# A new hand-written order for the first token group with its output layer, word buffers by need, and unmixed weight blocks sent to DRAM as soon as they are converted

## The chip, the cores and the metric

The kernel runs on one core of a Trainium2 chip, alone. A core has five engines, each of which works through its own instructions in order: TensorE (PE in the profile; PEld are its weight loads), VectorE (DVE), ScalarE (ACT), GpSimd (POOL) and SyncE (SP), which here only issues transfers (DMAs). They wait for one another by semaphores. The metric is the device time of one execution in microseconds (us).

## The reference

Inputs are q, k, v (float32) of 8 batches, 8 heads, 576 positions and 64 dimensions, and four weight matrices in float64. Attention runs within chunks of 64 positions; its output, as 4608 tokens of 512 features, goes through a layer that takes the largest of three products, and then through an output layer:

```python
scores = scale * np.matmul(q_c, k_c.transpose(0, 1, 2, 4, 3))
scores = scores - np.max(scores, axis=-1, keepdims=True)
attn = np.exp(scores)
attn = attn / (np.sum(attn, axis=-1, keepdims=True) + 1e-09)
out = np.matmul(attn, v_c)
...
h = np.maximum(np.maximum(x @ w1, x @ w2), x @ w3)
return (h @ w_out).astype(np.float32)
```

Here w1 to w3 are 512 x 768 and w_out is 768 x 512.

## The kernel before

**Tiles and groups.** The 4608 tokens are 36 tiles of 128. Two groups of four tiles come first (group 0 is tiles 0 to 3, group 1 is tiles 4 to 7), then four units of seven tiles. A float32 product is made of three reduced-precision ones (`three`, L154 to L157): each operand is split into a high part and the rest, and low times high, high times low and high times high are added in one PSUM bank. Three such matmuls are called a step.

**Groups 0 and 1** multiply plainly. The 768 hidden columns are six blocks j, each with three weights w; a block (j, w) is four steps over 512 tokens. After each of the three, the largest so far is kept (`maximum`, L289), and after the third the result is split (`high`, `low`, L297 and L303). The output layer (`onto`, L307) takes six steps for each tile, and `output` (L313) copies a tile out and stores it.

**The units** replace eight products by seven on operands that are sums of blocks. Their weights, nine sets (jp, w), are prepared once by `store` (L338): GpSimd adds high and low parts back together (L348) and forms four mixed blocks (L361), ACT and DVE split these (L366, L369), and SP writes one set as four transfers of unmixed blocks (`originals`, L371, 0.75 MB) and one of mixed blocks (`mixed`, L379, 1 MB). The units read them back through a ring.

**Attention of one tile** (`plain_steps`, L185) is a chain: load q and k (q), scores (S, PE, L205), maximum (mx, DVE, L210), subtract (sub, DVE, L215), exponential (exp, ACT, L219), sum (DVE, L163), add the small constant (eps, L166), reciprocal (rec, L169), normalize (nrm, DVE or GpSimd, L172), transpose (T, PE, L228), copy (at, ACT, L233), load v (v), times v (V, PE, L240), and for groups the split of the result (xh on ACT, L247; xl on DVE, L251). The scores of two tiles share one PSUM tile `s`, so S of a tile is held until sub of the tile before is done.

**Weights are converted** from float64 words on the chip. For each of 24 blocks (18 of w1 to w3 and six of w_out, which have j = 6) `piece` (L108) has seven operations: W loads 0.5 MB of words, A (ACT, L131) scales the upper word into a value buffer `ao`, B (ACT, L136) scales the lower word, C (DVE, L140) shifts, X (L144, DVE or GpSimd) adds, H (ACT, L147) takes the high part and Y (L150, DVE or GpSimd) the rest. X ends the use of the words, Y that of the value buffer.

**What sets the order.** The scheduler doesn't reorder: each engine gets its instructions in the order in which the program makes them. Group 0's hidden layer, all weight conversions and the attention of tiles 0 to 7 stand in the table `FIRST` (L44), one name for each operation: `q0`, `S0`, `T0` and so on for attention, `W01` for the words of block (0, 1), `h00a` for the product of block (0, 0) over columns 0 to 255 (b: 256 to 511, f: all), `F`, `hh` and `hl` for maximum, high and low, `i18` for 18 filler matmuls (L549). A `p` at the end puts the operation on GpSimd. Behind it, the output layer of group 0, group 1 and the units are loops of steps (L662 on); around these a planner places the remaining work by due times. `tiles` (L610) plans the attention of later tiles by `TABLE` (L32), and `stores` (L618) the nine sets, one each 7.2 us. `now` is its clock, which a step moves on by 0.68.

Of the kernel before, what the change touches and what calls it, by code (L numbers as in the profile page):

```python
# [20 lines left out]
P = 128  # L21
# [13 lines left out]
OPERANDS = 0.3  # L35

# [20 lines left out]
xh6 h52f F50f X65 X64p F51f H65 xh7 F52f H64 Y65 hh5f xl7 Y64 hl5f xl6
# [4 lines left out]
def chunk_attn_maxout_kernel(  # L62
# [44 lines left out]

    def piece(j, w):  # L108
# [18 lines left out]
        def exponent():  # L127


            st["a"] = ao_p.tile([P, 512], F32, name="ao", tag=f"ao{k % 4}")  # L130
            nc.scalar.activation(out=st["a"], in_=words(U32)[:, :, 1].bitcast(F32), func=AF.Prelu, scale=2.0 ** -112,  # L131
                                 alpha=2.0 ** 32)
# [52 lines left out]
    def plain_steps(t, x_of, col):  # L185
# [49 lines left out]
        def values():  # L235
            st["x"] = x = bank_of("ps_x")[:, :, t % 2] if t < 8 else bank_of("ps_s")[:, :, 1]
# [23 lines left out]
    def attention(t, x_of, col, norm):  # L260
# [3 lines left out]
        return [(at, pe, steps[name]) for name, at, pe in TABLE]  # L264
# [3 lines left out]
    def moe(t0, x_of, banks_in=((ps_m, "pm"),)):  # L268
# [386 lines left out]
    with tc.manual_schedule(engines={ET.PE, ET.DVE, ET.Activation, ET.Pool, ET.SP}):  # L655
# [4 lines left out]
        for g_ in groups:  # L660
            g_["places"][:] = places
# [46 lines left out]
```

## Time and profile before

| What | Value |
|---|---|
| median of 3 runs | 652.01 us (651.69 to 654.13) |
| the profiled execution | 654.27 us |
| its span, from first to last instruction | 652.5 us |
| granted TensorE clock, mean | 0.995 |
| moved by DMA | 133.70 MB, 205 GB/s over the span |
| median from issue to landing, q and k | 7.2 us |
| median from issue to landing, v | 6.7 us |
| median from issue to landing, mixed blocks | 5.1 us |
| group 0 with its output layer ends | 101.1 us |
| group 1's hidden layer ends | 170.8 us |

A line of the timeline gives start, duration, engine, line of the program, operation, what is written and read, and the count; in brackets the idle time before it and who ended that. A line of the view of waits gives who waited for whom, the total, the count and the longest. A line of the windows gives the stretch, its length, the busy time (and count) of PE, PEld, DVE, ACT and POOL, the granted clock, the share of the DMA engines and GB/s.

### The profile page before, as it was taken

To read this page: it belongs to the slowest core of one execution; us is meant where nothing else is said; L and a number is where in the kernel's file an instruction comes from. 1 tells how busy PE (TensorE), PEld (TensorE's weight loads), DVE (VectorE), ACT (ScalarE), POOL (GpSimd) and SP (SyncE) were. 2 spreads that over 40 slices of the span, in tenths; PEclk is the share of its full clock that TensorE was granted. 3 is DMA by queue.
4 is the path that set the end of the run, shared out by engine and by line. 5 is a ranking of instruction groups with operands and counts; after the bars stand their busy time and mean duration, and the time that the engine had idled before them with its cause. 6 is when DMAs were issued, how large, how long until landed. Compare 5 with 4: busy or idle time off the path is not lost.

```text
span 652.5 us, 12394 instructions
## 1 busy us (share of the span) xinstructions
PE 635.6 (97%) x5111; PEld 544.5 (83%) x5113; DVE 411.9 (63%) x667; ACT 235.0 (36%) x400; POOL 202.8 (31%) x179
## 2 busy tenths in 40 slices
PE   7899999889999999999999999999999999999997
PEld 3687888667889888888898898898989888999986
DVE  5897854588556767690585768348676761666520
ACT  5777733244332323352132424323242431112121
POOL 2431186675132323330323232123323321222200
PEclk9899999899999999999999999999999999999999
DMA  9844619998547575154576635346765341556311
GB/s 341 311 165 152 206 38 352 333 332 307 228 161 283 210 299 216 76 225 162 170 299 218 267 130 226 112 162 248 269 249 205 138 168 57 211 218 226 112 49 64
DMA packets 35911, 133.70 MB, mean 205 GB/s; under 512 B 3984, under 2 KB 6288, under 8 KB 30096
## 3 DMA queue, kind: packets, MB, share of 16 engines
q1 hardware_dynamic: 35856, 132.92, 55.1%
q8 instruction: 40, 0.66, 0.4%
q14 instruction: 15, 0.12, 0.1%
HBM read 106.95 MB, written 25.95 MB: 204 GB/s over the span
## 4 chain that ended last, share of the span: by engine, by line
PE 80%; DVE 8%; DMA 5%; ACT 4%; SPq 1%; issue 1%; POOL 0%; ACTq 0%; DVEq 0%
PE pm L155 25%; PE pm L156 24%; PE pm L157 24%; PE s L240 2%; PE s L205 2%; PE tp L228 2%; DMA buf<-in_vb 2%; DMA buf<-in_qk 1%; DMA w<-s 1%; DVE e L215 1%; DVE most L472 1%; DVE mx L210 1%; DVE pm L463 1%; DVE s L369 1%; DMA xl<-in_w 1%
## 5 line engine op out<-in xcount | busy, mean ns | idle before, releaser
L155 PE MATMUL pm<-X,ring 128*128 128x448 f32 x504 | 188.9, 375 | 0.0
L157 PE MATMUL pm<-X,ring 128*128 128x448 f32 x504 | 184.2, 365 | 0.0
L156 PE MATMUL pm<-X,ring 128*128 128x448 f32 x504 | 184.2, 365 | 0.0
L460 DVE TENSOR_TENSOR kept<-pm,kept 128x448 f32<-128x448 f32 x72 | 44.6, 620 | 101.4 <-PE pm L157 101.4
L466 POOL TENSOR_TENSOR kept<-kept 128x448 f32<-128x448 f32 x36 | 41.5, 1153 | 214.9 <-DVE kept L460 147.8
L155 PEld LDWEIGHTS pm<-X,ring 128*128 128x128 f32 x504 | 94.6, 188 | 8.8
L157 PEld LDWEIGHTS pm<-X,ring 128*128 128x128 f32 x504 | 94.7, 188 | 7.8
L156 PEld LDWEIGHTS pm<-X,ring 128*128 128x128 f32 x504 | 94.8, 188 | 7.1
L457 ACT COPY kept<-pm 128x448 f32<-128x448 f32 x72 | 38.3, 532 | 97.9 <-PE pm L157 94.0
L156 PE MATMUL pm<-wol,H 128*128 128x512 f32 x168 | 65.4, 389 | 0.0
L155 PE MATMUL pm<-woh,H 128*128 128x512 f32 x168 | 65.4, 389 | 0.0
L157 PE MATMUL pm<-woh,H 128*128 128x512 f32 x168 | 65.4, 389 | 0.0
L155 PE MATMUL pm<-xh,wl 128*128 128x512 f32 (+1 forms) x156 | 61.6, 395 | 0.0
L156 PE MATMUL pm<-xl,wh 128*128 128x512 f32 (+1 forms) x156 | 59.4, 381 | 0.3 <-DVE xl L251 0.3
L157 PE MATMUL pm<-xh,wh 128*128 128x512 f32 (+1 forms) x156 | 59.0, 378 | 0.0
L463 DVE TENSOR_TENSOR pm<-pm,kept 128x448 f32<-128x448 f32 x72 | 45.1, 626 | 12.4 <-PE pm L157 12.4
L172 POOL TENSOR_TENSOR e<-e,sm 128x512 f32<-128x512 f32 x23 | 24.1, 1046 | 71.6 <-DVE sm L169 48.0
L472 DVE TENSOR_TENSOR most<-pm,most 128x448 f32<-128x448 f32 x72 | 44.8, 622 | 2.2
L210 DVE TENSOR_REDUCE mx<-s 128x8 f32<-128x512 f32 x36 | 24.8, 688 | 31.2 <-ACT stage L254 24.6
L478 ACT CAST H<-most 128x448 fp32r<-128x448 f32 x48 | 26.9, 568 | 45.9 <-DVE most L472 45.7
L233 ACT COPY xs<-tp 128x512 f32<-128x512 f32 x36 | 21.1, 585 | 56.2 <-PE tp L228 56.2
L219 ACT ACTIVATE e<-e 128x512 f32<-128x512 f32 x36 | 22.8, 633 | 47.6 <-DVE e L215 47.6
(82 smaller groups left out, 969.7 us busy)
## 6 DMA issues: line engine op xcount, KB each, us to landing
ring<-w SPq DMA_DIRECT2D x36, 1024.0 KB, 6.7
ring<-w SPq DMA_DIRECT2D x36, 768.0 KB, 4.5
buf<-in_qk SPq DMA_DIRECT2D x36, 512.0 KB, 7.2
buf<-in_vb SPq DMA_DIRECT2D x36, 256.0 KB, 6.7
out_x<-ao SPq DMA_DIRECT2D x36, 256.0 KB, 2.1
w<-s SPq DMA_DIRECT2D x9, 1024.0 KB, 5.1
buf<-in_w SPq DMA_DIRECT2D x10, 512.0 KB, 3.8
buf<-in_wout SPq DMA_DIRECT2D x6, 512.0 KB, 3.4
```

The lines of the kernel that those rows point to most:

```text
L155: nc.tensor.matmul(out=o, lhsT=al, rhs=bh, start=first, stop=False)
L156: nc.tensor.matmul(out=o, lhsT=ah, rhs=bl, start=False, stop=False)
L157: nc.tensor.matmul(out=o, lhsT=ah, rhs=bh, start=False, stop=last)
L172: eng.tensor_tensor(out=e, in0=e, in1=sm.unsqueeze(2).broadcast_to([P, 8, 64]), op=ALU.mult)
L210: nc.vector.tensor_reduce(out=st["mx"].rearrange("p (g c) -> p c g", c=2), in_=st["s"], axis=AX.X, op=ALU.max)
L219: nc.scalar.activation(out=st["e"], in_=st["e"], func=AF.Exp, scale=SCALE)
L457: return lambda: nc.scalar.copy(out=kept(k), in_=o[i])
L460: return lambda: nc.vector.tensor_tensor(out=kept(k), in0=o[i], in1=kept(q), op=plus)
L463: return lambda: nc.vector.tensor_tensor(out=o[i] if w else M(j, c), in0=o[i], in1=kept(k), op=plus)
L466: nc.gpsimd.tensor_tensor(out=kept(2), in0=kept(2), in1=kept(1), op=plus)
L472: return lambda: nc.vector.tensor_tensor(out=M(j, c), in0=of(), in1=M(j, c), op=most)
L478: nc.scalar.copy(out=hh[j][:, c * half:(c + 1) * half], in_=M(j, c))
```

## The change

The program is changed in six places.

1. `FIRST` is another table. It loads q of tile 0 ahead of the first words, has 26 filler matmuls instead of 37, puts 23 operations on GpSimd instead of 17, and now holds the output layer of group 0 too (`P` with tile and block for its steps, `O` with the tile for the store), among the last blocks and the attention of tiles 5 to 7. `Z` opens the two further PSUM banks for products, which came only behind the table before; `M` starts the planner's work on the mixed sets.
2. `K` with a set's numbers writes the unmixed blocks of that set. It stands in the table, among the last weight blocks and the output steps; before, `store` planned it at 0.5 us into each set.
3. Word buffers: nine rooms, of which each W takes the first that is free in the table's order and each X gives one back (the rooms in the x tiles of group 1 only until those are needed). Before, the room was fixed by the block's number. Value buffers are handed out in the same way by A and Y.
4. Tiles 4 to 7 use the two halves of the bank pair `s` for S and for V, as later tiles do; before, they used the pairs `s` and `x` as tiles 0 to 3.
5. `LATER` moves T and at of the tiles that are prepared during group 1 by 1.4 us, and V and x by 2.8 us.
6. In the units, `high` and `low` of a finished block come 0.6 us later.

The planner's clock starts at -10.0 at `M` and runs on through the names P, S, T and V of the table. Nothing is added to or left out of the arithmetic.

```diff
+MIX = 0.5
+LATER = {"T": 1.4, "at": 1.4, "V": 2.8, "x": 2.8}
...
 FIRST = """
-W01 W02 q0 A01 C01 W10 A02 B02 C02 B01 q1 X02 i18 S0 X01 H02 q2 H01 Y02 A10 Y01p mx0 B10 sub0 q3 i5 S1 C10 exp0 sum0
...
+q0 i13 W01 A01 S0 i5 mx0 q1 sub0 W00 C01 exp0 sum0 S1 mx1 sub1 B01 q2 A00 exp1 W12 eps0 v0 q3 i8 rec0 B00 X01p S2 sum1
...
+P12 P33 xh6 xl6 P02 Y64 P13 Y65 P34 P14 P35 V7 P24 P03 K21 P25 P04 xh7 O2 P15 P05 K02 O0 xl7 O3 O1
...
+    words_in, values_in = {}, {}
+    free, rooms_of_words, x1 = list(range(9)), list(range(4)), False
+    for name in FIRST.split():
+        k = (3 * int(name[1]) + int(name[2])) if name[0] in "WAXY" else None
+        if name[0] == "W":
+            words_in[k] = free.pop(0)
+        elif name[0] == "A":
+            values_in[k] = rooms_of_words.pop(0)
+        elif name[0] == "Y":
+            rooms_of_words.append(values_in[k])
+        elif name[0] == "X":
+            free += [words_in[k]] if words_in[k] > 3 or not x1 else []
+        elif name[:2] == "xh" and int(name[2]) > 3 and not x1:
+            x1, free = True, [n for n in free if n > 3]
...
-            if k < 4 or 6 <= k < 10:
-                n = k if k < 4 else k - 6
-                st["r"] = early[n // 2][:, n % 2]
+            n = words_in[k]
+            if n < 7:
+                st["r"] = early[0][:, n] if n < 2 else early[1][:, n - 2] if n < 4 else early[2][:, n - 4]
             else:
-                st["r"] = att.tile([P, 512], I64, name="buf", tag="aa" if k in (20, 22) else ("qs", "rv")[k % 2], bufs=1)
+                st["r"] = att.tile([P, 512], I64, name="buf", tag=("qs", "rv")[n - 7], bufs=1)
...
-            st["s"] = s = bank_of("ps_s")[:, :, t % 2 if t < 8 else 0]
+            st["s"] = s = bank_of("ps_s")[:, :, t % 2 if t < 4 else 0]
...
-            st["x"] = x = bank_of("ps_x")[:, :, t % 2] if t < 8 else bank_of("ps_s")[:, :, 1]
+            st["x"] = x = bank_of("ps_x")[:, :, t % 2] if t < 4 else bank_of("ps_s")[:, :, 1]
...
-        return [(at, pe, steps[name]) for name, at, pe in TABLE]
+        return [(at + later.get(name, 0.0), pe, steps[name]) for name, at, pe in TABLE]
...
-        return [(0.0, whole(0, a)), (1.1, whole(1, b)), (0.5, originals), (2.2, sum_of(0, a21, a22, plus)),
+        ops[f"K{jp}{w}"] = originals
+        return [(0.0, whole(0, a)), (1.1, whole(1, b)), (2.2, sum_of(0, a21, a22, plus)),
...
-                return ops + ([(at + 0.8, high(j, c)), (at + 1.7, low(j, c))] if w == 2 else [])
+                return ops + ([(at + 1.4, high(j, c)), (at + 2.3, low(j, c))] if w == 2 else [])
...
+    early.append(stage_p.tile([P, 3, 512], I64, name="stage"))
...
+    for tt in range(4):
+        for j in range(JT):
+            ops[f"P{tt}{j}"] = lambda a=(tt, j): g0["onto"](*a)
+        ops[f"O{tt}"] = lambda tt=tt: g0["output"](tt)
+    mixing = [store(n) for n in range(len(sets))]
...
+            elif name == "Z":
+                more_banks()
+            elif name == "M":
+                running = True
+                stores()
             else:
                 ops[name]()
+            if running and name[0] in "PSTV":
+                passed(STEP)
...
-    groups, parts = [g0], [("do", lambda: stores()), ("steps", lambda: g0["project"](0, 1, 2, 3, before=4))]
+    groups, parts = [g0], []
...
-                for at, pe, fn in attention(t0 + tt, stage, tt * P, nc.gpsimd if u else nc.vector):
+                for at, pe, fn in attention(t0 + tt, stage, tt * P, nc.gpsimd if u else nc.vector, {} if u else LATER):
...
-            for at, fn in store(n):
-                plan(now + 6.0 + 7.2 * n + at, 0.0, fn)
+            for at, fn in mixing[n]:
+                plan(now + MIX + 7.2 * n + at, 0.0, fn)
...
-    now = -4 * JT * STEP - 2.0
+    now = -10.0
```

**The start of the program.** SP's first transfers before the change (`xh` and `xl` are rooms for words in the x tiles, `in_qk` holds q and k of a tile, `in_vb` its v):

```order
L122 DMA xh_128<-in_w123 128x512
L122 DMA xl_129<-in_w123 128x512
L193 DMA buf_137<-in_qk 128x1024
L122 DMA xl_129<-in_w123 128x512
L193 DMA buf_148<-in_qk 128x1024
L193 DMA buf_189<-in_qk 128x1024
L193 DMA buf_201<-in_qk 128x1024
```

and after it:

```order
L211 DMA buf_136<-in_qk 128x1024
L140 DMA xh_128<-in_w123 128x512
L211 DMA buf_180<-in_qk 128x1024
L140 DMA xh_128<-in_w123 128x512
L211 DMA buf_210<-in_qk 128x1024
L140 DMA xl_129<-in_w123 128x512
L215 DMA buf_217<-in_vb 128x512
```

The first q moved from third place to the first, one word block comes between each two loads of q, and v of tile 0 comes ahead of the fourth q. GpSimd's first work on weights and attention before (`ao` is a value buffer, `e` the exponentials of a tile, `sm` their sums; L144 is X, L150 is Y, L172 is nrm):

```order
L150 TENSOR_TENSOR wl0_120<-ao_139,wh0_114 128x512
L144 TENSOR_TENSOR ao_193<-ao_193,xl_129 128x512
L144 TENSOR_TENSOR ao_296<-ao_296,xh_128 128x512
L172 TENSOR_TENSOR e_316<-e_316,sm_343 128x512
L150 TENSOR_TENSOR wl1_121<-ao_193,wh1_115 128x512
```

and after (L162 is X, L190 nrm, L168 Y):

```order
L162 TENSOR_TENSOR ao_153<-ao_153,xh_128 128x512
L190 TENSOR_TENSOR e_182<-e_182,sm_187 128x512
L190 TENSOR_TENSOR e_207<-e_207,sm_249 128x512
L162 TENSOR_TENSOR ao_212<-ao_212,xh_128 128x512
L190 TENSOR_TENSOR e_266<-e_266,sm_319 128x512
L168 TENSOR_TENSOR wl0_120<-ao_212,wh0_114 128x512
```

All of the first three tiles' normalizations are GpSimd's now, where tiles 0 and 1 were DVE's, and the low part of block (0, 0), which stood on DVE, is sixth in its row.

**Group 1.** SP's transfers around the loads of q for tiles 8 and 9 before (`w1_1243`, `w2_1305` and `w3_1388` are sets in DRAM, `s_1288` mixed blocks, `out_x` the output):

```order
L193 DMA buf_1272<-in_qk 128x1024
L317 DMA out_x<-ao_1274 128x512
L374 DMA w2_1305<-wh0_114 128x512
L374 DMA w2_1305<-wl0_120 128x512
L376 DMA w2_1305<-wh1_115 128x256
L376 DMA w2_1305<-wl1_121 128x256
L380 DMA w1_1243<-s_1288 128x2048
L197 DMA buf_1320<-in_vb 128x512
L193 DMA buf_1330<-in_qk 128x1024
L374 DMA w3_1388<-wh2_116 128x512
L374 DMA w3_1388<-wl2_122 128x512
```

and after:

```order
L335 DMA out_x<-ao_1281 128x512
L211 DMA buf_1288<-in_qk 128x1024
L399 DMA w1_1029<-s_1301 128x2048
L215 DMA buf_1328<-in_vb 128x512
L211 DMA buf_1338<-in_qk 128x1024
L399 DMA w2_1269<-s_1371 128x2048
```

The unmixed blocks (L374 and L376) are gone from this stretch. On TensorE, the scores and the transpose around one tile of group 1 stood side by side before (`s<-buf` is S, `tp<-ident` is T, `s<-xs` is V):

```order
L205 MATMUL s<-buf 64x64 x16
L228 MATMUL tp<-ident,e 128x128 x4
L155 MATMUL pm<-xh,wl_122 128x512
L156 MATMUL pm<-xl,wh_116 128x512
L157 MATMUL pm<-xh,wh_116 128x512
```

and after, V and the scores of two tiles on stand side by side, and T comes three steps later:

```order
L258 MATMUL s<-xs,buf 64x64 x16
L223 MATMUL s<-buf 64x64 x16
L173 MATMUL pm<-xh,wl_122 128x512
L174 MATMUL pm<-xl,wh_116 128x512
L175 MATMUL pm<-xh,wh_116 128x512
```

T, which stood right behind S of the next tile, now has three steps ahead of it, and V comes four steps behind T instead of three.

More of the change, by code (lines that the diff above doesn't have):

```diff
@@ L35 @@
 OPERANDS = 0.3
+MIX = 0.5
+LATER = {"T": 1.4, "at": 1.4, "V": 2.8, "x": 2.8}
 FIRST = """
-W01 W02 q0 A01 C01 W10 A02 B02 C02 B01 q1 X02 i18 S0 X01 H02 q2 H01 Y02 A10 Y01p mx0 B10 sub0 q3 i5 S1 C10 exp0 sum0
-X10p W00 S2 mx1 eps0 sub1 v0 rec0 exp1 nrm0 sum1 i8 T0 v1 S3 mx2 at0 eps1 A00 rec1 nrm1 q4 B00 C00 i6 T1 sub2 V0 at1
-exp2 W12 mx3 X00p sum2 V1 xh0 W21 eps2 rec2 H10 sub3 nrm2p H00 xl0 v2 S4 xh1 Y00 exp3 Y10p xl1 W20 A12 T2 sum3 B12
-h00a eps3 v3 rec3 at2 C12 nrm3 A21 h01a B21 q6 C21 A20 X12 T3 V2 at3 W11 C20 H12 B20 X21 W30 V3 xh2 Y12p mx4 F00a xl2
@@ new lines @@
+H01 mx2 eps1 nrm0p T0 at0 rec1 v1 sub2 nrm1p V0 T1 exp2 C00 S3 X00p xh0 q4 W02 at1 B12 sum2 H00 eps2 V1 rec2 mx3 xh1
+nrm2p sub3 T2 S4 xl0 exp3 xl1 sum3 at2 Y00p v2 B02 W10 eps3 rec3 v3 nrm3 A02 W20 h00a V2 A12 C02 W31 T3 Y01p A10 xh2
+X02 H02 at3 C10 W11 C12 X12p F00a h01a Y02 V3 xl2 B10 xh3 B31 q5 X10p xl3 A20 W21 A11 h02a F01a H12 F02a B11 C11 W61
+W52 Z B20 B21 W40 H10 mx4 sub4 hh0a exp4 W22 C20 X20 W32 Y12 X11 Y10 A31 H11 W30 h01b hl0a h00b C31 h02b A21 H20 X31
+S5 F00b C21 Y11 h12f F01b A40 q6 v4 H31 sum4 W41 B40 X21p h10f F02b H21 Y31 Y20 B30 hh0b eps4 hl0b Y21 C40 mx5 B61
@@ L282, in products @@
             xh, xl = x_of()
-            ps[j, w] = bank()
+            ps[j, w, lo] = bank()
             for ct in range(CT):
-                three(ps[j, w][:, :n], wh[j][:, w, ct, :], wl[j][:, w, ct, :], xh[:, ct, cols], xl[:, ct, cols],
+                three(ps[j, w, lo][:, :n], wh[j][:, w, ct, :], wl[j][:, w, ct, :], xh[:, ct, cols], xl[:, ct, cols],
                       ct == 0, ct == CT - 1)
@@ L330, in hidden @@
                 [(1.1, lambda: high(j, 0, 512)), (1.8, lambda: low(j, 0, 512))] if w == 2 else [])
-        return dict(products=products, maximum=maximum, high=high, low=low, hidden=hidden, project=project, places=places)
+        return dict(products=products, maximum=maximum, high=high, low=low, hidden=hidden, project=project, places=places,
+                    onto=onto, output=output)
     minus, plus, most = ALU.subtract, ALU.add, ALU.max
@@ L555, in first_group @@
     def first_group():
+        nonlocal now
+        running = False
         for name in FIRST.split():
@@ L562, in first_group, with passed @@
                 ops[name](nc.vector)
+            elif name == "Z":
[3 more added lines that the diff above has]
+                stores()
             else:
                 ops[name]()
+            if running and name[0] in "PSTV":
+                passed(STEP)
     due = []
+    def passed(step):
+        nonlocal now
+        now += step
+        while due and due[0][0] <= now:
+            _, _, pe, fn = heapq.heappop(due)
+            fn()
+            now += pe
     def plan(at, pe, fn):
@@ L667, in chunk_attn_maxout_kernel @@
                 step, after = after if isinstance(after, tuple) else (STEP, after)
-                now += step
                 for at, fn in after:
-                    plan(now + at, 0.0, fn)
-                while due and due[0][0] <= now:
-                    _, _, pe, fn = heapq.heappop(due)
-                    fn()
-                    now += pe
+                    plan(now + step + at, 0.0, fn)
+                passed(step)
         while due:
```

35 lines of the change are left out of this document (17 added, 18 removed).

## The prediction

> **What bounds the kernel now.** I read the page's engine and clock lines first, then the view of who waited for whom, for TensorE alone, in two stretches.
>
> ```profile
> PE 635.6 (97%) x5111; PEld 544.5 (83%) x5113; DVE 411.9 (63%) x667; ACT 235.0 (36%) x400; POOL 202.8 (31%) x179
> PEclk9899999899999999999999999999999999999999
> ```
>
> TensorE is the bound: it is busy for 97% of the span, and the next engine for 63%. The clock digits dip to 8 twice, in the second slice and the eighth (a slice is 16.3 us). Time can only come from the places where TensorE idles, runs at a lower clock or does filler work. The waits from 0 to 101 us come first, those from 100 to 172 us behind the dots; what waits there are later lie in stages that the change leaves in their order.
>
> ```profile
> PE s L205 <- DVE e L215: 3.3, 3, 1.6
> PE pm L549 <- DVE h L551: 1.5, 1, 1.5
> PE tp L228 <- DVE e L172: 1.2, 2, 0.6
> PE tp L228 <- POOL e L172: 1.1, 1, 1.1
> ...
> PE s L205 <- DMA buf<-in_qk: 2.5, 1, 2.5
> PE tp L228 <- DVE e L172: 1.9, 2, 1.4
> ```
>
> The columns are total, times and longest. Scores (S, L205) and transposes (T, L228) wait for the softmax chain; the 1.5 us of L549 is the start of the program; one S waits 2.5 us for a transfer. These waits sum to 11.5 us, so they aren't all: filler and clock come on top. The landmarks and the pace of TensorE come from its timeline.
>
> ```profile
> 1.46 5.88 PE L549 MATMUL pm<-h 128*128 128x512 bf16 x18 [1.46 <-DVE h L551]
> ...
> 22.68 0.58 PE L156 MATMUL pm<-xl,wh 128*128 128x256 f32 x1 [0.28 <-DVE xl L251]
> 30.98 0.69 PE L205 MATMUL s<-buf 64*64 64x64 f32 x32 [0.56 <-DVE e L215]
> 31.61 0.38 PE L155 MATMUL pm<-xh,wl 128*128 128x256 f32 x1
> 32.26 0.28 PE L155 MATMUL pm<-xh,wl 128*128 128x256 f32 x1
> 32.61 0.28 PE L155 MATMUL pm<-xh,wl 128*128 128x256 f32 x1
> 37.81 0.50 PE L155 MATMUL pm<-xh,wl 128*128 128x512 f32 x1
> 44.75 0.39 PE L155 MATMUL pm<-xh,wl 128*128 128x512 f32 x1
> 45.43 0.39 PE L155 MATMUL pm<-xh,wl 128*128 128x512 f32 x1
> 60.32 0.66 PE L228 MATMUL tp<-ident,e 128*128 128x128 f32 x4 [1.07 <-POOL e L172]
> 60.73 0.48 PE L155 MATMUL pm<-xh,wl 128*128 128x512 f32 x1
> 101.06 0.39 PE L155 MATMUL pm<-xh,wl 128*128 128x512 f32 x1
> 170.81 0.39 PE L155 MATMUL pm<-woh,h 128*128 128x512 f32 x1
> ```
>
> The columns are start and duration; many rows between are left out. Starts show the pace, since matmuls overlap: a step of three products costs 45.43 - 44.75 = 0.68 us at 512 columns (a block of four steps 2.72) and 0.35 at 256 (a half block 1.4); an S costs 0.63 (30.98 to 31.61), and V, with the same 32 small matmuls, is taken alike; a T costs 0.41 (60.32 to 60.73). The first half block runs from 22.68, the full blocks of group 0 from 37.81, group 1 from 101.06, and its output layer from 170.81.
>
> From 22.68 to 37.81 the work is 6 half blocks (8.4), two S and three V (3.15) and two T (0.8): 12.4 us in 15.1. From 37.81 to 101.06 it is 15 blocks and 24 output steps (84 steps, 57.1), one S, three V and three T (3.75): 60.9 in 63.3, so only 2.4 is lost there, 1.1 of it the POOL wait and 1.3 the cost of seven insertions, 0.2 each. From 101.06 to 170.81 it is 72 steps (49.0) and seven tiles' S, V and T (11.7): 60.7 in 69.8. Nearly all that can be won lies **before 37.81 and between 101 and 171**.
>
> **Term 1: the start, up to the first half block.** The same work precedes it in both kernels (S0 to S4, T0 to T2, V0, V1); the order and the suppliers change. The rows that price the chain:
>
> ```profile
> 4.45 0.67 ACT L131 ACTIVATE ao<-xh 128x512 f32<-128x512 f32 x1 [2.44 <-DMA xh<-in_w]
> 8.12 1.03 PE L549 MATMUL pm<-h 128*128 128x512 bf16 x4 [0.16 <-issue]
> 8.88 0.68 DVE L210 TENSOR_REDUCE mx<-s 128x8 f32<-128x512 f32 x1
> 9.60 0.69 DVE L215 TENSOR_TENSOR e<-s,mx 128x512 f32<-128x512 f32 x1
> 10.33 0.63 ACT L219 ACTIVATE e<-e 128x512 f32<-128x512 f32 x1 [0.35 <-DVE e L215]
> 10.35 1.16 PE L205 MATMUL s<-buf 64*64 64x64 f32 x64 [1.21 <-DVE e L215]
> 10.99 0.69 DVE L163 TENSOR_REDUCE sm<-e 128x8 f32<-128x512 f32 x1 [0.36 <-ACT e L219]
> 19.92 0.20 DVE L169 RECIPROCAL sm<-sm 128x8 f32<-128x8 f32 x1
> 20.29 1.04 POOL L172 TENSOR_TENSOR e<-e,sm 128x512 f32<-128x512 f32 x1 [1.49 <-DVE sm L169]
> 28.64 1.29 POOL L150 TENSOR_TENSOR wl<-ao,wh 128x512 fp32r<-128x512 f32 x1 [5.62 <-ACT wh L147]
> ```
>
> The first transfer, a weight block, lands at 4.45. Now the first is q0, of the same size, so S0 waits only for its fillers: 13 instead of 18, which ended at 1.46 + 5.88 = 7.34. The last five run at full pace (four in 1.03 with their overlap, some 0.22 each): 7.34 - 1.1 = 6.2 for S0. Each link of the softmax chain takes 0.72 (mx to sub, 8.88 to 9.60), 0.73 (sub to exp), 0.66 (exp to sum) and 0.75 (sub to the next S, as S1 waits for sub0); S to mx I take as 0.76. By hand through the DVE's new order: S1 8.4; sum0 9.1, mx1 9.7, sub1 10.4; S2 11.2; sum1 11.8, mx2 12.4, rec1 13.2.
>
> Then GpSimd carries the path. Its new order there is X01p, nrm0p, nrm1p, X00p, nrm2p, Y00p: three normalizations (1.04 each; two of them were the DVE's) and three conversion steps (1.29 each). X01p starts near 9.6 behind B01, nrm0p at 11.5; nrm1p follows rec1 by 0.37 (19.92 to 20.29) at 13.6; X00p ends at 15.9, nrm2p at 17.0, Y00p at 18.3. The first half block needs Y00's low words, so it can start at **18.3**; xl1 on the DVE is due at the same time. I take 18.7, for collisions between DVE and GpSimd. Before, the order made it wait until 22.68, so the gain is **4.0**. Bounds: 4.7 with nothing in the way; 2.7 if each of the six GpSimd steps is late by 0.2.
>
> **Term 2: 18.7 to the full blocks.** Six half blocks (8.4), S5, T3, V2 and V3 (2.3) and four insertions (0.8) make 11.5, plus 0.7 for a slow clock, which the row below shows for before as well: at 72% of 5 us, 1.4 us of pace went missing.
>
> ```profile
> 20.00:25.00 5.00, 3.99 (x48) 3.49 (x49) 4.79 (x12) 4.56 (x9) 2.73 (x2) 0.72 0.93 323
> ```
>
> That is 12.2, to 30.9. From there 84 steps (57.1), two S, four V and four T (5.4) and ten insertions (2.0) make 64.5: **95.4**. For waits that the trace can't show (the conversions of ACT and DVE stay close behind TensorE, output steps stand between the last blocks, tiles 4 to 7 share one bank pair) I add 1.0, from bounds of 0 and 4.0; 4.0 is over twice the 1.6 of softmax waits (0.56, 1.07) that the old order had after its first half block. Group 0 with its output ends at **96.4 instead of 101.06: 4.7**. The five banks that Z opens early can only take waits away. Word buffers by need cost no instruction; W21 to W30 are issued once a conversion frees a room, by my walk 5 us or more before ACT wants them, so that queue hides itself, as long as a transfer lands in some 5 us.
>
> **Term 3: group 1.** Seven tiles are prepared here while nine mixed weight sets are written to DRAM.
>
> ```profile
> 105.00:110.00 5.00, 5.00 (x52) 3.95 (x51) 1.30 (x2) 1.06 (x1) 4.66 (x5) 1.00 1.05 370
> 115.00:120.00 5.00, 2.50 (x40) 1.96 (x39) 1.46 (x3) 0.00 (x0) 3.90 (x4) 0.78 1.03 405
> 108.76 0.92 SPq L193 DMA_DIRECT2D buf<-in_qk  x1
> 118.17 1.13 PE L205 MATMUL s<-buf 64*64 64x64 f32 x32 [2.50 <-DMA buf<-in_qk]
> 119.23 1.11 PE L228 MATMUL tp<-ident,e 128*128 128x128 f32 x4
> 121.34 0.39 PE L155 MATMUL pm<-xh,wl 128*128 128x512 f32 x1
> ```
>
> The DMA engines are full (share 1.03 to 1.05), and q9, issued at 108.76, holds S9 until 118.17: 2.5 us idle. The clock then drops: S, T and one step take 121.34 - 118.17 = 3.17 where they should take 1.72, so 1.45 more. Per tile, one set brings 0.75 MB of unmixed blocks, 1 MB of mixed ones and 0.75 MB of q and v. The change writes the unmixed blocks in group 0, so 0.75 of 2.5 MB goes: at 370 GB/s a tile's transfers fall from 6.8 to 4.7 us, below its seven-microsecond share of the stretch. In SP's queue q9 then has only w1 and v8 ahead of it. I take all 3.95. LATER puts T 1.4 us and V 2.8 us later, which removes the T waits (1.9, longest 1.4); behind a waiting T stand only matmuls with operands at hand; the load of v for the tile after next shares V's buffer and now waits for V in SP's queue, about 1 us, with the next q behind it. That gives 5.85; I keep 5.0, as one wait of some 0.9 may come back (the loads of q have little lead). Bounds: 1.9, if q9 is late anyway, and 5.85.
>
> The unmixed blocks now stand in SP's queue between the last word and v loads: nine times four transfers, 6.75 MB or 18 us at 370 GB/s, beside some 10 us for what else moves there, in about 30 us. Nothing computed waits for them, and TensorE's own work hides them; without that cover, 0 to 18 us.
>
> In the units, high and low now come 0.6 us later. Before the output layer reaches those rows 12 steps (8.2 us) pass, so that costs 0.
>
> **Sum.** 4.7 + 5.0 = 9.7. From the profiled span of 652.5 that gives 642.8; the execution lasted 654.27, 1.8 beyond its span, and the median of the runs is 652.01. Against that median I predict **642.3**.
>
> **Rivals.** *Conversions bind group 0:* DVE is busy for 4.79 of 5 us in the row from 20 to 25. If ACT and DVE can't keep up when TensorE starts earlier, the 4.7 shrinks to about 1.0: 652.0 - 6.0 = 646.0. Against it: each word block's instructions are the same, and six more of them, net, run on GpSimd.
>
> *The clock in the start:* 11 fillers go (37 to 26). After the last one at 10.8 TensorE has some 4.5 us of work in 8. If it then runs slow for most of that, S takes 1.06 as at 118.17 (to 119.23) instead of 0.63 and T is drawn out alike, some 2.5 more for the chain to 18.7, and the first half block about 1.1: 645.9. [...]
>
> *The transfers don't thin out:* the mixed blocks and q still meet, and q9 is late. Group 1 then gains only 1.9: 652.0 - 6.6 = 645.4.
>
> *Slower: loads behind the stores.* v6, W62 and v7 now stand behind unmixed blocks in SP's queue. v7 can be issued once V5 has freed its buffer and is needed some 13 us later, by the steps between. If the stores' 18 us all run ahead of it and it then takes the 9.4 us that q9 took (108.76 to 118.17), V7 and the output steps behind it come 18 + 9.4 - 13 = 14.4 us late: 656.7. The sign turns where the delay passes 9.7, that is once v7 lands over 23 us after V5. Against it: five of the nine sets are issued before V5 runs.
>
> **How the numbers follow.** Forecast 0.60, conversions 0.15, clock 0.10, transfers 0.08, slower 0.05; 0.02 is left for the change not doing what it says (652). About 0.5%, or 3.3 us, is what a measurement of this kernel can tell from no change. Forecast, clock and transfers are faster; conversions mostly; a mix of two of them reaches "same": faster 0.86, same 0.09, slower 0.05. The range takes the upper bounds (term 1 0.7 more, waits 1.0 less, clock 0.7 less, group 1 0.85 more: 639.1) and below it half a microsecond, and on the other side two half-failed terms (term 1 1.3 less, waits 3.0 more, group 1 1.9 less: 648.5): **638.5 to 648.5**.
>
> **What would show it.** Right: first half block at 18 to 19.5 us, first group 1 step at 95 to 98, no wait of S for in_qk and T waits under 0.5 in group 1, its output layer starting near 161. Wrong: waits of TensorE on ACT's or DVE's conversions that sum to over 3 us in group 0; a clock below 0.8 in several windows before 25 us; q9 landing over 8 us after its issue; V7 waiting for in_vb.

## The result, and the profile after

| | before | after |
|---|---|---|
| median | 653.07 us (4 runs, 651.69 to 654.97) | **643.35 us** (4 runs, 642.90 to 643.64) |
| profiled execution | 654.27 us | 643.22 us |
| its span | 652.5 us | 641.4 us |

The change makes the kernel 1.5% faster: the ratio is 0.985, with a 95% interval from 0.982 to 0.988. The prediction of 642.3 us was 1.1 us too low, and its range holds the time. (The median of before is of four runs here, one more than the prediction had.)

The page of after, its lines on engines and on the granted clock:

```profile
PE 630.0 (98%) x5102; PEld 541.1 (84%) x5102; DVE 410.2 (64%) x661; ACT 234.8 (37%) x400; POOL 213.9 (33%) x185
PEclk9999999999999999999999999999999999999999
```

TensorE is the bound as before, with nine instructions fewer (11 fillers went), and the two dips of the clock are gone. The view of who waited for whom, for TensorE, first from 0 to 100 us, then (last line) from 95 to 165:

```profile
PE tp L246 <- POOL e L190: 1.9, 2, 1.2
PE pm L576 <- DVE h L578: 1.5, 1, 1.5
PE x L258 <- ACT xs L251: 0.7, 1, 0.7
PE s L223 <- DVE e L233: 0.5, 2, 0.4
PE pm L174 <- DVE xl L269: 0.3, 1, 0.3
...
PE s L223 <- DMA buf<-in_qk: 2.8, 3, 1.3
```

Total, times and longest, as before. The waits of S for the softmax (3.3 us) are down to 0.5, those of T in group 1 (1.9) are gone, and what is left in group 1 are three waits of S for a load of q. The landmarks, from TensorE's timeline of after:

```profile
19.74 0.28 PE L174 MATMUL pm<-xl,wh 128*128 128x256 f32 x1
...
31.84 0.50 PE L173 MATMUL pm<-xh,wl 128*128 128x512 f32 x1
...
95.96 0.39 PE L173 MATMUL pm<-xh,wl 128*128 128x512 f32 x1
...
104.77 0.69 PE L223 MATMUL s<-buf 64*64 64x64 f32 x32 [1.17 <-DMA buf<-in_qk]
...
146.66 0.69 PE L223 MATMUL s<-buf 64*64 64x64 f32 x32 [1.32 <-DMA buf<-in_qk]
...
161.67 0.39 PE L173 MATMUL pm<-woh,h 128*128 128x512 f32 x1
...
177.99 0.36 PE L173 MATMUL pm<-X,ring 128*128 128x448 f32 x1
```

They are, in order, the first half block (the row that answers to 22.68), the first full block (37.81), group 1 (101.06), two scores that wait, group 1's output layer (170.81) and the first product of the units. Where the 11.1 us between the spans went follows from these rows. A second profile of before, e8 below, stands beside, since the first had slow clock in it:

| Stage | before | before again (e8) | after | gain predicted | gain to before / to e8 |
|---|---|---|---|---|---|
| to the first half block | 22.68 | 23.00 | 19.74 | 4.0 | 2.9 / 3.3 |
| from there to group 1 | 78.38 | 76.61 | 76.22 | 0.7 | 2.2 / 0.4 |
| group 1, hidden layer | 69.75 | 68.99 | 65.71 | 5.0 | 4.0 / 3.3 |
| group 1, output layer | 16.32 | 16.32 | 16.32 | 0 | 0 / 0 |
| units to the end | 465.4 | 464.7 | 463.4 | 0 | 2.0 / 1.3 |
| span | 652.5 | 649.6 | 641.4 | 9.7 | 11.1 / 8.2 |

By medians the gain is 9.7, between the two columns: as the sum said, but **not from the stages it said**. The 1.1 us by which the forecast was too low is the amount by which the fourth run moved the median of before.

### The profile page after: what moved, and what is told of

The parts are those of the page before. It is cut to its first block, busy times and chain, and to the rows that moved or that the text cites. A ratio compares the mean times of both kernels' runs of the same rounds, so it can differ in the third digit from the quotient of the medians.

```text
span 641.4 us, 12371 instructions
## 1 busy us (share of the span) xinstructions
PE 630.0 (98%) x5102; PEld 541.1 (84%) x5102; DVE 410.2 (64%) x661; ACT 234.8 (37%) x400; POOL 213.9 (33%) x185
## 4 chain that ended last, share of the span: by engine, by line
PE 92%; DVE 4%; DMA 2%; ACT 1%; issue 0%; SPq 0%; ACTq 0%; DVEq 0%
PE pm L173 29%; PE pm L174 27%; PE pm L175 27%; PE s L258 3%; PE s L223 3%; PE tp L246 2%; DMA buf<-in_qk 2%; PE pm L576 1%; DVE e L233 1%; DVE mx L228 1%; DVE s L388 1%; DVE sm L181 1%; DVE xl L269 0%; DVE sm L184 0%; ACT s L385 0%
## 5 line engine op out<-in xcount | busy, mean ns | idle before, releaser
L190 POOL TENSOR_TENSOR e<-e,sm 128x512 f32<-128x512 f32 x26 | 27.3, 1051 | 71.5 <-DVE sm L187 51.5
L251 ACT COPY xs<-tp 128x512 f32<-128x512 f32 x36 | 21.1, 585 | 52.0 <-PE tp L246 51.9
L498 ACT CAST H<-most 128x448 fp32r<-128x448 f32 x48 | 26.8, 568 | 29.4 <-DVE most L492 29.0
```

Source lines behind the costliest of these rows:

```text
L190: eng.tensor_tensor(out=e, in0=e, in1=sm.unsqueeze(2).broadcast_to([P, 8, 64]), op=ALU.mult)
L498: nc.scalar.copy(out=hh[j][:, c * half:(c + 1) * half], in_=M(j, c))
```

## The experiments

All are edits of after unless it says otherwise. The median of before differed by 0.7 us from chip to chip (653.01 to 653.73), so an effect of a microsecond on the time is read together with its landmark, and less than that from the landmark alone. Landmarks of the start have a scatter of their own: in the eight profiles whose start is that of after (after, e1, e2, e3, e6, e7, e10, e11), S0 starts at 5.66 to 7.11. From S0 to the first product of group 0 it then takes 12.84 to 12.86 us in all eight, so an edit of the start is read from S0 on.

**e8: the kernel before, unchanged, profiled once more.**

> The kernel before once more, for its profile: its times spread from 650.9 to 655.5 us while the changed kernel's spread by 0.7. Theory (the start's and q9's stalls and the clock behind them vary): the landmarks differ by 1 us or more from the first profile at the first half block (22.0), at the full blocks (37.8) or at group 1's end (170.8), and the units' pace (277.2 - 187.1 = 90.1 for the first) is the same within 0.2. Rival (the units vary): landmarks up to 170.8 agree within 0.7 us and the units differ.

Measured: 651.41 us, span 649.6. Two rows of its timeline (group 1's first step, a score that waits) and its window from 115 to 120 us, where the clock stands third from the end:

```profile
99.61 0.39 PE L155 MATMUL pm<-xh,wl 128*128 128x512 f32 x1
116.11 0.69 PE L205 MATMUL s<-buf 64*64 64x64 f32 x32 [1.88 <-DMA buf<-in_qk]
115.00:120.00 5.00, 3.89 (x77) 3.15 (x78) 1.89 (x4) 2.06 (x3) 2.49 (x2) 1.00 1.02 402
```

The clock is at 1.00 here and also from 20 to 25 us, where the first profile had 0.78 and 0.72. The waits of group 1 are the same in kind and size (2.6 us for q against 2.5, T 1.9 in both). So 2.9 of the 11.1 us between the profiles are a difference between two executions of the same kernel, not the change, most of it in stages where the first one's clock dipped. The profile of e4, which has the old start too, dips again (0.81 from 20 to 25 us, 0.84 from 25 to 30) and takes 78.2 us from the first half block to group 1, as the first did (78.4), where the undipped one takes 76.6.

**e1: unmixed blocks written as before, by the planner, at 0.5 us into each set.**

```diff
-... K11 ... K00 ... K12 ... K01 ... K22 ... K20 ... K10 ... K21 ... K02 ...
-        ops[f"K{jp}{w}"] = originals
-        return [(0.0, whole(0, a)), (1.1, whole(1, b)), (2.2, sum_of(0, a21, a22, plus)),
+        return [(0.0, whole(0, a)), (1.1, whole(1, b)), (0.5, originals), (2.2, sum_of(0, a21, a22, plus)),
```

> The changed kernel, but the unmixed blocks are planned with their sets again, 0.5 us into each, as before the change; everything else stays. Theory (thinner transfers are what group 1 gains from): the loads of q are late again, the waits of S for in_qk in group 1 rise from 2.8 us to 5 or more, perhaps with a drop of the clock, and group 1 (65.7 us in the changed kernel) takes 68 to 70; the time rises from 643.4 to 646 to 648. Rival (LATER alone makes the room, the transfers were hidden): group 1 stays within 0.7 us of 65.7 and the time within 1 us of 643.4. In both, group 0 ends at 96.0, give or take 0.5, or up to 1 earlier if the stores had slowed it.

Measured: 644.98 us (644.73 to 645.38), ratio 0.988 (0.985 to 0.991); group 1 takes 67.0 us, 1.3 more than with the early blocks, and the time is 1.6 more. One score of its timeline, two rows of SP's queue (a load of v, and the load of q that this score needs) and the window around it:

```profile
141.42 0.69 PE L223 MATMUL s<-buf 64*64 64x64 f32 x32 [3.00 <-DMA buf<-in_qk]
131.82 0.33 SPq L215 DMA_DIRECT2D buf<-in_vb  x1
...
134.76 0.42 SPq L211 DMA_DIRECT2D buf<-in_qk  x1
140.00:145.00 5.00, 3.58 (x47) 3.03 (x48) 2.77 (x4) 1.11 (x2) 4.84 (x6) 1.00 1.07 410
```

Four transfers of unmixed blocks stand between the two SP rows; in after that load is issued at 132.65. The blocks delay q, and S waits, as term 3 has it; the worth is between what the two theories gave.

**e4: the other way round, before with its unmixed blocks written early.** All nine sets are planned at the start of the output layer of group 0, 0.3 us apart; nothing else of the change.

```diff
-        return [(0.0, whole(0, a)), (1.1, whole(1, b)), (0.5, originals), (2.2, sum_of(0, a21, a22, plus)),
+        plan(now + 0.1 + 0.3 * n, 0.0, originals)
+        return [(0.0, whole(0, a)), (1.1, whole(1, b)), (2.2, sum_of(0, a21, a22, plus)),
```

> The kernel before, with one thing changed: all unmixed blocks are planned at the start of group 0's output layer (0.3 us apart), where its DMA engines were idle. Theory (thinner transfers): q9 lands in time, the 2.5 us wait and the 1.45 us of slow clock behind it go, time 3 to 4 us below the kernel before (652 to 653), that is 648 to 650, with the T waits in group 1 (1.9 us) still there. Rival (q9 is late for the mixed blocks and its own 0.5 MB): less than 1 us below. If the stores' issues on SP hold up the first loads of q behind them, it may gain less: S of tile 8 would show that wait.

Measured: 649.67 us (9 runs, 648.56 to 651.18), ratio 0.994 (0.992 to 0.996), 3.4 us less than before. TensorE's waits in group 1, the whole answer:

```profile
PE tp L228 <- DVE e L172: 1.9, 2, 1.4
PE s L240 <- issue: 0.4, 1, 0.4
```

No S waits for q any more, the T waits stand untouched, and group 1 takes 66.2 (101.05 to 167.27), 2.8 less than in e8. This one part of the change, in the old order, gives a third of the whole gain.

What it does to q of tile 9 can be read from SP's queue and the time from issue to landing. Before, that load was issued at 108.76 (a row of the prediction), 7.7 us behind group 1's first step, and landed after 9.3 us. Here it is issued at 104.98, 3.9 us behind that step, and lands after 8.4; in after the figures are 100.89, 4.9 and 8.2. So without the blocks in the queue the **issue** comes 3.8 us earlier (2.8 in after), while the flight is shorter by only 0.9 (1.1).

**e2: T, at, V and x of group 1 at their old times.**

```diff
-LATER = {"T": 1.4, "at": 1.4, "V": 2.8, "x": 2.8}
+LATER = {}
```

> The changed kernel with LATER empty: T and V of the tiles prepared in group 1 at their old places. Theory (the DVE's normalization was late for T): TensorE waits on T for the DVE again, 1 to 2 us in group 1, and the time rises by 1 to 2 us to 644.4 to 645.4. Rival (the T waits came from the delays that the late q had left behind): no T waits over 0.5 us, time within 0.7 us of 643.4.

Measured: 644.53 us (644.25 to 644.83), ratio 0.987 (0.985 to 0.990); group 1 takes 67.6, 1.9 more, the time 1.2 more. Its waits from 95 to 165 us:

```profile
PE tp L246 <- DVE e L190: 1.9, 2, 1.4
PE s L223 <- DMA buf<-in_qk: 1.3, 1, 1.3
```

The T waits return to the digit, and the waits for q fall from 2.8 to 1.3. So LATER removes 1.9 and **gives some of it back as a later q**.

**e11: e1 and e2 together.** The edits are those two.

> The changed kernel with both of the parts that act on group 1 undone: the unmixed blocks planned with their sets and LATER empty. Undone one at a time they cost group 1 1.3 us (67.0 instead of 65.7) and 1.9 us (67.6). Theory (the two are all that group 1 gained from): group 1 takes 68.5 to 70, as in the kernel before (69.0 and 69.8), and the time is 646 to 647.5. Rival (they overlap, or the new order of group 0 helps group 1 as well): group 1 takes less than 68.2.

Measured: 644.69 us (644.26 to 646.33), ratio 0.986 (0.982 to 0.990); group 1 takes 67.65, the sum of its waits is 2.6 for q and 0.8 for T. In group 1 the two parts are worth 1.3 and 1.9 alone and 1.95 together. By medians of the time it is 1.6, 1.2 and 1.3; the profile here is of the slowest of the four executions (646.33), so 67.65 may be high. Either way **they overlap**. That a tile that waits for the one gets slack for the other would explain it, but is not shown. With both undone group 1 is still 1.3 us shorter than the 69.0 of e8; that remainder comes with the rest of the change, and which part does it was not found.

**e7: q ahead of the stores and earlier, meant to beat both.** The last three unmixed sets move ahead of the load of v7, which takes them out of the start of group 1, and each load of q in group 1 is planned 1.5 us earlier.

```diff
-LATER = {"T": 1.4, "at": 1.4, "V": 2.8, "x": 2.8}
+LATER = {"q": -1.5, "T": 1.4, "at": 1.4, "V": 2.8, "x": 2.8}
...
-... K20 F51f ... v7 ... H64 K10 P23 ... P03 K21 P25 ... P05 K02 O0 ...
+... K20 K10 K21 K02 F51f ... v7 ... H64 P23 ... P03 P25 ... P05 O0 ...
```

> Meant to beat the changed kernel: the three last sets of unmixed blocks go ahead of the load of v for tile 7 in SP's queue, where the DMA engines were idle from 70 to 80 us, and q of the tiles prepared in group 1 is planned 1.5 us earlier, so that it stands ahead of the load of v that waits for V. Theory (the 2.8 us of waits for in_qk that the changed kernel has in group 1 are the queue's): waits of S for in_qk in group 1 fall to 0.6 us or less, group 1 takes 63 to 64 us instead of 65.7, time 640.6 to 641.8. Rival (the transfers themselves are slow, beside the mixed blocks): waits of 1.5 us or more stay, time above 642.5.

Measured: **640.15 us** (639.99 to 640.49), ratio 0.981 (0.978 to 0.983), 3.2 less than after. Rows of its timeline, group 1's first step and the first of its output layer:

```profile
96.04 0.39 PE L173 MATMUL pm<-xh,wl 128*128 128x512 f32 x1
...
158.47 0.39 PE L173 MATMUL pm<-woh,h 128*128 128x512 f32 x1
```

Group 1 takes 62.4, 3.3 less, and TensorE waits for nothing there; both are a little better than the theory asked. So the 2.8 us of q waits that after has left come from what stands ahead of q in SP's queue. Rows of it in after, up to the loads of q whose S waits for 1.17 and for 1.32 us (L335 stores output, L399 mixed blocks, L215 loads v), with two lines of what SP waited for from 95 to 165 us:

```profile
97.56 1.41 SPq L335 DMA_DIRECT2D out_x<-ao  x3
99.02 0.73 SPq L211 DMA_DIRECT2D buf<-in_qk  x1
...
138.32 0.33 SPq L215 DMA_DIRECT2D buf<-in_vb  x1
139.32 0.33 SPq L399 DMA_DIRECT2D w<-s  x1
139.74 0.38 SPq L211 DMA_DIRECT2D buf<-in_qk  x1
...
SPq L399 <- DVE s L388: 20.5, 5, 6.2
SPq L215 <- PE s L258: 17.7, 5, 5.2
```

The first of these loads stands behind the last set of unmixed blocks (issued from 95.16 on) and the output of group 0. The other stands behind a load of v, which waits until a V has freed its buffer, and behind mixed blocks, which wait for the DVE's split (L388); SP shows no wait for a buffer of q itself. In e7 the first load of q is issued at 98.22 instead of 99.02 and the last at 131.52 instead of 139.74. For the last, that is 8 us of lead, beside which its faster landing (the last loads take 5.8 and 6.9 us) is small. The first gains 0.8 us by its issue and 1.9 by its landing (3.8 us instead of 5.7), with the last set of stores no longer moving then. The two edits of e7 were not separated.

**e9: the normalizations of tiles 0 and 1 back on DVE.**

```diff
-... mx2 eps1 nrm0p T0 at0 rec1 v1 sub2 nrm1p V0 ...
+... mx2 eps1 nrm0 T0 at0 rec1 v1 sub2 nrm1 V0 ...
```

> The changed kernel with the normalizations of tiles 0 and 1 on the DVE again. Theory (the start gains because GpSimd takes work off the DVE): the DVE, which then carries 1.2 us more between sub1 and xl1, delivers sum2, rec2 and xl1 later, and the first half block starts at 20 to 21 us instead of 19.5; the time rises by 0.5 to 1.5 us. Rival (the start gains from the order alone; GpSimd's 1.04 us a tile is slower than the DVE's 0.69, and it shuts out the DVE's small steps meanwhile): the first half block starts at 18.5 to 19.5 and the time is the same or up to 0.7 us less.

Measured: 643.89 us (643.67 to 644.01), ratio 0.984 (0.981 to 0.988). A new line among TensorE's waits, and the first product of group 0:

```profile
PE tp L246 <- DVE sm L187: 2.0, 1, 2.0
...
21.44 0.38 PE L173 MATMUL pm<-xh,wl 128*128 128x256 f32 x1
```

That product stood at 19.52, 1.9 us earlier. S0 starts later here too, at 7.11 instead of 6.67, and from S0 on 14.33 us pass instead of 12.85. So the move of the two normalizations to GpSimd **shortens the start by 1.5 us**. The time hardly shows it (0.5 us more by medians, nothing by the ratio), because group 1 falls from 65.7 to 64.5 (its q waits from 2.8 to 1.7): of the later start, 1.2 us come out of a wait that stood behind it anyway.

**e5: the fillers behind S0 and S1 left out (13 of 26).**

```diff
-q0 i13 W01 A01 S0 i5 mx0 q1 ... v0 q3 i8 rec0 ...
+q0 i13 W01 A01 S0 mx0 q1 ... v0 q3 rec0 ...
```

> The changed kernel without the 5 and 8 filler matmuls between S0 and S2 (the first 13 stay). The changed kernel granted the full clock in every window up to 165 us, against the 0.7 us that the prediction took for a slow clock and against the rival that fewer fillers cost 3 us. Theory A (the remaining S, T and V keep the clock up by themselves, S1 and S2 wait for the DVE and not for fillers): the first half block starts at 19.5, give or take 0.7, no window below 0.95, time within 1 us of 643.4. Theory B (the 13 fillers are what still keeps it up): one or two windows of the first 30 us show 0.6 to 0.85, the first half block starts 1 to 3 us later, time 645 to 648.

Measured: 644.09 us (643.54 to 644.70), ratio 0.986 (0.983 to 0.990). Two of its windows and a row of its timeline, T of tile 0:

```profile
10.00:15.00 5.00, 1.95 (x40) 1.41 (x44) 4.09 (x11) 2.91 (x6) 3.30 (x3) 0.80 1.02 409
15.00:20.00 5.00, 5.00 (x108) 4.10 (x111) 3.28 (x7) 3.71 (x7) 3.58 (x4) 0.51 0.49 185
...
13.07 1.11 PE L246 MATMUL tp<-ident,e 128*128 128x128 f32 x4 [0.74 <-POOL e L190]
```

The clock falls to 0.51, as the clock rival had it, yet the first half block starts only 1.0 us later (its first product at 20.56, with S0 at 6.70) and the time is 0.7 more. T takes 1.11 instead of 0.66 us but starts where it starts in after (13.05): it waits for GpSimd in both. The slow TensorE added its own few tenths (0.45 us at this T) to a chain that the other engines carry. The 13 fillers are worth 0.7 to 1.0 us, not the rival's 3.6.

**e6: the two further PSUM banks opened late.** `Z` stands just ahead of the first output step.

```diff
-... W61 W52 Z B20 ... F42f P10 ...
+... W61 W52 B20 ... F42f Z P10 ...
```

> The changed kernel with Z, which opens two more PSUM banks for products, just ahead of the first output step instead of ahead of the second half blocks, so that all of group 0's hidden layer has three banks, as before the change. Theory (banks are no limit there, maxima follow their products in time): group 0's end within 0.7 us of 96.0 and time within 1 us of 643.4. Rival (a good part of group 0's 5.1 us comes from the banks): waits of products for ACT or DVE (the copies and maxima) of 2 us or more in group 0, time 645 or more.

Measured: 645.59 us (645.46 to 647.29), ratio 0.990 (0.987 to 0.992). The first full block in its timeline:

```profile
34.47 0.50 PE L173 MATMUL pm<-xh,wl 128*128 128x512 f32 x1 [2.11 <-ACT m L311]
```

It waits 2.1 us for ACT to take the first maximum out of a bank, a wait that neither kernel has; group 0 ends at 98.8, and the time is 2.2 more: the rival's case, not the theory's. Fewer banks with the new order would have been **a new wait in the place of an old one**.

**e10: the output layer of group 0 behind its hidden layer, as before.** All `P` and `O` go to the end of the table, in the old order of tiles, with the planner's clock set so that the mixed sets keep their places.

```diff
-... P10 ... P30 ... P20 ... P31 ... P15 P05 K02 O0 xl7 O3 O1
+... K02 xl7 P00 P01 P02 P03 P10 ... P33 P04 P05 O0 P14 P15 O1 P24 P25 O2 P34 P35 O3
...
-MIX = 0.5
+MIX = 7.3
...
-    now = -10.0
+    now = -16.8
```

> The changed kernel with all output steps of group 0 behind its hidden layer and the attention of tiles 5 to 7, as a block in the old order of tiles; the planner's clock is set so that the mixed sets come at the same distance from group 1. Theory (the output steps between are what covers the chains of tiles 5 to 7): TensorE waits 2 to 6 us on T and V of these tiles, group 0 ends at 98 to 102 instead of 96.0, time 645.5 to 649.5. Rival (those chains have long been done by then): waits under 1 us, group 0's end within 0.7 us of 96.0.

Measured: 649.28 us (6 runs, 648.52 to 650.23), ratio 0.993 (0.990 to 0.995). Two rows of its timeline and two of its windows:

```profile
80.13 0.63 PE L246 MATMUL tp<-ident,e 128*128 128x128 f32 x4 [2.54 <-ACT xs L251]
81.88 1.13 PE L258 MATMUL s<-xs,buf 64*64 64x64 f32 x32 [1.13 <-DVE xl L269]
...
80.00:85.00 5.00, 2.31 (x56) 1.92 (x60) 3.57 (x6) 2.71 (x5) 2.49 (x2) 0.61 1.07 396
85.00:90.00 5.00, 5.00 (x39) 4.00 (x32) 2.51 (x4) 1.64 (x2) 4.77 (x6) 0.71 0.10 30
```

Group 0 ends at 103.1 instead of 96.0, later than the theory's 98 to 102. T and V of tiles 5 to 7 wait for each other's chain with nothing between them, and the clock falls on top. The output steps are what covers that end; without them this order is **5.9 us slower**. That isn't a share of the 9.7: the kernel before also had its output layer last, but in its order TensorE waits for no T or V from 61.5 us to the end of group 0.

**e3: high and low in the units at their old times.**

```diff
-... [(at + 1.4, high(j, c)), (at + 2.3, low(j, c))] ...
+... [(at + 0.8, high(j, c)), (at + 1.7, low(j, c))] ...
```

> The changed kernel with high and low of a finished block in the units at their old places (0.8 and 1.7 instead of 1.4 and 2.3). From the end of group 1 on the changed kernel took 1.9 us less than the kernel before, which the prediction had put at 0. Theory (the split stood ahead of the copy behind T on ACT): the V waits on ACT (1.0 us) and some 0.9 us more come back, the units take 1.5 to 2 us longer, time 645 to 645.4. Rival (the units gain from another phase of the loads or of the clock): units within 0.4 us of the changed kernel's, time within 0.7 us of 643.4.

Measured: 644.73 us (644.17 to 645.55), ratio 0.988 (0.985 to 0.991). A line of TensorE's waits from 165 us on, where after has none:

```profile
PE s L258 <- ACT xs L251: 1.0, 3, 0.3
```

The wait of V for ACT's copy is back, and the units take 464.7 us (178.62 to the end of the 643.3), as in e8, against 463.4; 1.3 us is a little under the theory's 1.5 to 2. Why, ACT's timeline shows at the first of the three, in e3 and then in after (L251 is `at`, L498 `high`):

```profile
241.34 0.57 ACT L498 CAST H<-most 128x448 fp32r<-128x448 f32 x1 [0.50 <-DVE most L492]
241.82 0.58 ACT L251 COPY xs<-tp 128x512 f32<-128x512 f32 x1
...
239.83 0.58 ACT L251 COPY xs<-tp 128x512 f32<-128x512 f32 x1
240.31 0.57 ACT L498 CAST H<-most 128x448 fp32r<-128x448 f32 x1
```

In e3 the copy stands behind a split that waits for DVE; 0.6 us later in the plan, the split stands behind the copy.

## Why the prediction held, and where it didn't

**The start (4.0 predicted; 2.9 and 3.3).** The mechanism was right: GpSimd carried the path in the order that the prediction walked through, and e9 prices its share in the gain at 1.5 us. The size was off, at the sentence that took 18.7 "for collisions between DVE and GpSimd". By the walk 12.1 us pass from S0 (6.2) to the first half block (18.3), and it allowed 0.4 on top; 12.85 passed. (Its bound of 4.7 "with nothing in the way" is a slip: 22.68 - 18.3 is 4.4.) Rows of GpSimd, then of DVE, in after:

```profile
13.99 1.04 POOL L190 TENSOR_TENSOR e<-e,sm 128x512 f32<-128x512 f32 x1 [1.00 <-DVE sm L187]
15.45 1.30 POOL L162 TENSOR_TENSOR ao<-ao,xh 128x512 int32<-128x512 int32 x1 [0.42 <-ACT e L237]
17.18 1.04 POOL L190 TENSOR_TENSOR e<-e,sm 128x512 f32<-128x512 f32 x1 [0.43 <-PE x L258]
...
13.45 0.16 DVE L184 TENSOR_SCALAR sm<-sm 128x8 f32<-128x8 f32 x1
14.42 0.90 DVE L158 TENSOR_SCALAR ao<-ao 128x512 uint32<-128x512 uint32 x1
15.99 0.79 DVE L184 TENSOR_SCALAR sm<-sm 128x8 f32<-128x8 f32 x1
```

S0 starts at 6.67 instead of 6.2, well within its scatter, so nrm1p at 13.99 instead of 13.6. Then C00 (L158) takes 0.90, most of it beside nrm1p, and ends at 15.32; X00p needs it (the bracket names an exponential that ended 0.1 us earlier and that X00p doesn't read); the small constant of tile 2 (L184) takes 0.79 instead of 0.16 and ends with X00p, at 16.8; nrm2p, at 17.18, needs the reciprocal behind it (its bracket names a V whose result it doesn't read). The walk priced the GpSimd steps at their durations and let each start on time; two of the DVE steps between them took longer beside GpSimd's own, 0.90 us where another C took 0.42 with GpSimd idle (at 8.77), and 0.79 instead of 0.16.

**From there to group 1 (0.7; 2.2 and 0.4).** The walk had 12.2 us from the first half block to the first full block and 65.5 from there to group 1; they took 12.1 and 64.1. The 0.7 for slow clock wasn't needed, as the clock stayed at 1.00, and of the 1.0 for waits only 0.3 came. Of the 2.2 us against the first profile of before, 1.8 are what that profile was slower than e8. That output steps cover the end of group 0 holds in this order (e10). "The five banks that Z opens early can only take waits away" holds too, but the walk, which counts no wait for a bank, rests on it: with three banks the new order waits for one and takes 2.2 us more (e6).

**Group 1 (5.0; 4.0 and 3.3).** Both causes are real: the blocks (e1, e4) and T's place (e2). Two steps failed. One **added them**: 3.95 for the blocks, 1.9 for T, one wait of 0.9 back. They overlap (e11), and not one wait for q came back but three, 2.8 us in all. The prediction did name the reason for the last two of these (1.6 us), a load of v that waits for V with the next q behind it, and undersized it; the first (1.2 us) stands behind stores. The other step was the measure, a tile's transfers at 370 GB/s: what made q early or late was mostly its time of issue (q of tile 9 in e4, 3.8 us against 0.9 of flight; the last q in e7, 8 us), though the first q of e7 gained more by landing faster (1.9 us against 0.8). In after the q of tile 9 even takes 8.2 us to land, over the 8 that the prediction gave as a sign that it was wrong, and its S waits for nothing.

**The units (0; 2.0 and 1.3).** The prediction looked for a cost of the later split and found it covered. It missed the gain: TensorE's three waits of V for ACT's copy go, and e3 gets 1.3 us back with them. They stood in the view of waits before, from 165 us on, a stretch that the prediction left aside as unchanged:

```profile
PE s L240 <- ACT xs L233: 1.0, 3, 0.3
```

The other 0.7 us against the first profile of before is again what that one was slower than e8.

**The unmixed blocks in SP's queue** were covered, as predicted: V7 starts at 91.11 without a wait. **Rivals:** conversions didn't bind (TensorE waits 0.3 us for an xl and for no weight). The clock didn't fall in after (a mean of 1.000); in e5, where it fell to 0.51, the start took 1.0 us longer, of the 3.6 that the rival asked. The slower case, loads behind the stores, didn't come for v7; a weaker form of it came for the first q of group 1.

Of the signs that the prediction gave for being right, group 1's start (95.96) and end (161.67) and the missing T waits came; the first half block was just late (19.74 for 18 to 19.5), and S did wait for q. That the sum came out to a tenth by medians is luck. Against the first profile of before, 1.1 us too much in the start and 1.0 in group 1 stand against 1.5 and 2.0 too little in the other two stages; against e8, 0.7, 0.3 and 1.7 too much stand against 1.3 too little, and the gain is 8.2. The word buffers alone, and the bank halves of tiles 4 to 7 alone, were not tried.

## What to carry to other kernels

In this kernel a transfer that waited for its buffer or its data held the later ones of the same queue (in after, from 95 to 165 us, SP waited 17.7 us for buffers of v and 20.5 us for mixed blocks, with loads of q behind both): put the one that is needed first ahead of it, and look at a transfer's time of issue before thinning the traffic. Don't add the gains from two waits of the same stage before both have been tried together. An edit that takes one part out of a new order prices what that order needs, which isn't what the part added to the old one. Before an edit that only moves work by a fraction of a microsecond is set to nothing, look at the small waits of its own stage, for they may be what it removes.

## What the hardware showed that was not expected

**The same idle didn't always cost clock.** 2.50 us of idle in the first profile of before was followed by a granted clock of 0.78 in that window; 1.88 us at nearly the same place in e8, and 3.00 us in e1, were not (1.00). In e10 gaps of 2.54, 1.13 and 1.43 us within seven microseconds came with 0.61 and 0.71. So the clock fell in two of the four cases, and not in the one with the longest gap (3.00 us). What sets the cases apart no run here shows. Nor is it shown that the dips make the spread of before (3.3 us over its four runs, against 0.7 for after). They go with it: of its 28 runs beside the experiments, the seven with a mean clock of 0.999 or 1.000 took 650.9 to 652.7 us, the others 651.6 to 656.3. But two runs of e9 at 0.996 were no slower than two at 1.000.

**Small adds on DVE lasted as long as the GpSimd operation beside them.** An add of 128 x 8 elements took 0.16 us alone and 0.79 beside a GpSimd operation, ending when that ended; eight of the 36 adds of after took 0.56 to 1.15 us, each beside one, and the other 28 at most 0.17. The sums over 128 x 512 beside it kept their 0.69. Why the add is held and the sum isn't, no run here shows. Where such a step of 0.16 us stood in the chain, it cost 0.6 us.
